# Attention, gated unit and rational unit on one core: the matrices of batches 3 to 7 from half-precision parts of the weights

## The chip, the cores and the metric

One core of one Trainium2 chip runs the whole kernel. The metric is the device time of one execution in microseconds; a kernel's time is the median of its runs.

## The reference, cut to what matters

There are 8 batches of 8 heads with 576 rows of 64, 32 packing rows a head, a gated unit of width 1536 and a second unit of width 2048.

```python
p_packed = sm_attn(p, k, v)                # 32 rows a head
out = sm_attn(q, p_packed, p_packed)       # 576 rows a head
x = transposed out                          # 4608 x 512
xn = x / rms * rms_g
g, val = xn @ w_gate, xn @ w_val           # 512 x 1536 each
x = silu(g) * val @ w_out                  # 1536 x 512
h = x @ w_in                               # 512 x 2048
out = (P(h) / (Q(h) + 1e-6)) @ w_out2      # polynomials in h; 2048 x 512
```

Since the second attention only mixes the 32 packed rows of each head, a row of x is a row of weights (8 heads x 32) times the packed rows. The kernel therefore multiplies the packed rows with `w_gate` and `w_val` once a batch and applies the attention's weights to the products. These products are what the kernel calls the matrices of a batch.

## The kernel before

Most products are taken in three passes in half precision: each operand is a high part and a low part (`PASSES`: high by high, high by low, low by high), summed in PSUM. The 64-bit inputs of the weights are decoded into single precision by three VectorE instructions (L129, L133, L135, the steps wB, wC and wD).

The work of a batch is written as short steps with names, and a list of names fixes the order in which every engine gets its instructions. `START` (L904) holds batches 0 and 1; `BLOCK` (L959) is run for b = 2 to 6 (L1233) and joins the gated unit of batch b with the attention and the matrices of batch b + 1; batch 7 has a loop of its own (L1253). The second unit follows. TensorE's queue and the others are served in the order of the list.

The steps that matter here:

- G and V followed by half and column (`gv_mm`, L982): a projection, six half-precision matmuls into one of five PSUM tiles of the pool `ps_m`. A is the tanh (ScalarE, L1001), D and E are the two products (VectorE, L1005 and L1008), which read and so free the tiles of G and V; Y and Z are the high and low part of the result (ScalarE L1015, GpSimd L1020).
- O followed by half, column group and third (`o1_mm`, L1049): the product with `w_out`; P, Q and S evict and store it.
- hk, hv, hq are casts of the next batch's inputs (ScalarE, L700), lk, lv, zq their low parts (VectorE L709 or GpSimd L707).
- bA and bD write the packed rows of a batch as high and low parts into `pkz` (L785, L791); bM (`pk_gain`, L800) writes them once more in single precision, times the gain of the norm, into `pkm` by four small VectorE instructions (L260).
- M0 to Mb (`m_mm`, L380) are the 12 items of the matrices. An item takes 512 columns of `w_gate` or `w_val` and 128 rows of two weight tiles. Its two matmuls write the two halves of 64 partitions of a PSUM tile, and both operands are in single precision:

```python
for i_ in range(2):
    nc.tensor.matmul(
        out=ps[64 * i_:64 * i_ + 64, :], lhsT=pkm[g][:, i_, :], rhs=wgv[nm, fr, 2 * g + i_], start=True, stop=True
    )
```

  MA and MD (L388, L393) take an item out of PSUM as a high part (ScalarE, L391) and a low part (VectorE, L396).
- wB to wL prepare the 32 weight tiles of the second unit: wL loads a raw tile (ScalarE's queue, one of three buffers), wB, wC, wD decode it, wA scales (L1184) and wH casts (L1188) on ScalarE, wP takes the low part on GpSimd (L1192), wS stores both parts to DRAM on ScalarE's queue. `w2.start()` (L1232) issues the first three loads ahead of block 2. Seven tiles are done in each of blocks 2 and 3 and six in each of blocks 4 to 6.

In `BLOCK`, the steps of TensorE around the M items stand in this order (M0, M2, M4, the five from M1 to M7, M8 M9 and Mb Ma are six groups):

```text
G13 M0 V13 M2 G14 V14 G15 V15 G16 bm1 V16 G17 M4 V17 M1 M3 M5 M6 M7 G18 V18 ... G1b M8 M9 V1b Mb Ma O100
```

A first-attention step (L588) multiplies in single precision, s1a (L732) and xo (L853) multiply in half precision with 64 columns in places.

Of the kernel before, what the change touches and what calls it, by code (L numbers as in the profile page):

```python
# [9 lines left out]
F32 = mybir.dt.float32  # L10
F16 = mybir.dt.float16
I32 = mybir.dt.int32
I64 = mybir.dt.int64
AF = mybir.ActivationFunctionType
ALU = mybir.AluOpType
# [5 lines left out]
PASSES = ((0, 0), (0, 1), (1, 0))  # L21
S_QKP = 2.0**4
S_V = 2.0**7
S_A = 2.0**12
S_PK = 2.0**10
S_AN = 2.0**5
S_M = 2.0**13
# [3 lines left out]
S_WI2 = 2.0**10  # L31
S_G = 2.0**4
S_WO2 = 2.0**11
# [3 lines left out]
def attention_pack_glu_rational_kernel(  # L37
# [16 lines left out]
    nc = tc.nc  # L54
# [5 lines left out]
    KC = DM // 128  # L60
# [17 lines left out]
    act = nc.scalar.activation  # L78
    stt = nc.vector.scalar_tensor_tensor
# [6 lines left out]
    const = sb("const", "left")  # L86
    st_p = sb("stage", "left")
# [12 lines left out]

    g_raw = const.tile([128, KC], F32, name="g_raw")
    g_sc = const.tile([128, KC], F32, name="g_sc")
    g_first = const.tile([128, KC], F32, name="g_first")
    m_half = const.tile([128, 2], F32, name="m_half")
    ab = const.tile([128, 6], F32, name="ab")
# [3 lines left out]
    wgv = {}  # L109
# [54 lines left out]
    def place1(nm, fr, kc):  # L164
        t = wgv[nm, fr, kc] = gv_p.tile([128, 512], F32, name=f"w{nm}_{fr}_{kc}")
        return t

    w1 = Weights(w_items, place1)
    w1_dec = w1.steps()
# [24 lines left out]
    m_items = [(fr, nm, g) for fr in range(DFF // 512) for nm in "gv" for g in range(2)]  # L194
# [14 lines left out]
    pkz = [at_p.tile([128, 2, 4, 64], F16, name=f"pkz{g}") for g in range(2)]  # L209

    pkm = [at_p.tile([128, 2, 64], F32, name=f"pkm{g}") for g in range(2)]
# [3 lines left out]
    pT = at_p.tile([128, 2, 4, 64], F16, name="pT")  # L215
# [161 lines left out]
    def matrices(b, st):  # L377


        def m_mm(i):  # L380
            fr, nm, g = m_items[i]
            ps = st["mm", i] = ps_m.tile([128, 512], F32, tag="m", name="mm")
            for i_ in range(2):
                nc.tensor.matmul(  # L384
                    out=ps[64 * i_:64 * i_ + 64, :], lhsT=pkm[g][:, i_, :], rhs=wgv[nm, fr, 2 * g + i_], start=True, stop=True
                )

        def m_hi(i):  # L388
            fr, nm, g = m_items[i]
            t = mt[b, nm, fr, g] = mt_p.tile([128, 2, 512], F16, tag="mt", bufs=MTB, name="mt")  # L390
            act(out=t[:, 0], in_=st["mm", i], func=AF.Copy, scale=1.0)  # L391

        def m_lo(i):  # L393
            fr, nm, g = m_items[i]
            t = mt[b, nm, fr, g]
            stt(  # L396
                out=t[:, 1], in0=st["mm", i], scalar=1.0, in1=t[:, 0], op0=ALU.mult,
                op1=ALU.subtract,
            )

        def m_less(i):
            fr, nm, g = m_items[i]
            for i_ in range(2):
                nc.tensor.matmul(
                    out=st["mm", i][64 * i_:64 * i_ + 64, :], lhsT=minus[:, 64 * i_:64 * i_ + 64],
                    rhs=mt[b, nm, fr, g][:, 0], start=False, stop=True,
                    skip_group_check=True,
                )

        def m_rest(i):  # L410
            fr, nm, g = m_items[i]
            act(out=mt[b, nm, fr, g][:, 1], in_=st["mm", i], func=AF.Copy)

        pieces = {}
        for i in range(len(m_items)):
            for nm, f in (("M", m_mm), ("MA", m_hi), ("MD", m_lo), ("MP", m_less), ("ML", m_rest)):
                pieces[f"{nm}{i:x}"] = lambda f=f, i=i: f(i)
        return pieces
# [221 lines left out]
    def attention(b):  # L640
# [316 lines left out]
        "+MAa +MDa"  # L957
    )
    BLOCK = (  # L959
# [19 lines left out]
    )  # L979


# [162 lines left out]
    def norms():  # L1144
        nc.vector.tensor_scalar_mul(minus, ident, -1.0)
        nc.vector.tensor_scalar_mul(g_sc, g_raw, S_M / (S_A * S_V))
        nc.vector.tensor_scalar_mul(g_first, g_raw, S_M / S_A)

    def constants():
# [10 lines left out]
    w2_items = []  # L1160
# [4 lines left out]
        w2_items.append(("o", 0, kc, w_out2[kc * 128:(kc + 1) * 128, :]))  # L1165
    w2_dram = {it[:3]: tc.dram_tile((128, 2, 512), F16, name="w2{}_{}_{}".format(*it[:3])) for it in w2_items}
    w2t = {}
    kept = []

    def place2(nm, fr, kc):  # L1170

        raw = w2.raw[[it[:3] for it in w2_items].index((nm, fr, kc))]
        t = raw.bitcast(F16)[:, 0:1024].rearrange("p (a t) -> p a t", a=2)
        kept.append(((nm, fr, kc), t))
        return t, S_WI2 if nm == "i" else S_WO2

    w2 = Weights(w2_items, place2)

    w2_done = []

    def w2_scale():
        w2_done.append(w2.dec.pop(0))
        nm = w2.items[len(w2_done) - 1][0]
        act(out=w2_done[-1], in_=w2_done[-1], func=AF.Copy, scale=S_WI2 if nm == "i" else S_WO2)  # L1184

    def w2_hi():
        t, _ = place2(*w2.items[w2.n][:3])
        act(out=t[:, 0], in_=w2_done[-1], func=AF.Copy)  # L1188

    def w2_lo():  # L1190
        t = kept[-1][1]
        nc.gpsimd.tensor_tensor(out=t[:, 1], in0=w2_done[-1], in1=t[:, 0], op=ALU.subtract)  # L1192
        w2.n += 1

    def w2_store():
        key, t = kept.pop()
        nc.scalar.dma_start(out=w2_dram[key], in_=t)

    w2_dec = w2.steps()

    def w2_pieces(b):
        todo = {nm: lambda: next(w2_dec) for nm in ("wB", "wC", "wD")}
        todo |= {"wA": w2_scale, "wH": w2_hi, "wP": w2_lo, "wS": w2_store, "wL": w2.load}
        return {f"{nm}{j}": f for nm, f in todo.items() for j in range(7 if b < 4 else 6)}

    w2_p = None
    w2_left = list(w2_items)
# [14 lines left out]
    ctx.enter_context(tc.manual_schedule())  # L1222
    steps = {"-" + nm: f for nm, f in attention_first().items()}
    steps |= attention(1) | block(0) | w1_pieces() | blanks() | {"cc": norms, "cd": constants}
    steps |= {"+" + nm: f for nm, f in (attention(2) | block(1) | w2_pieces(1)).items()}
    for nm in START.split():
        steps[nm]()
    an.pop(0)
# [2 lines left out]
        ys.pop((b, h, c))  # L1231
    w2.start()  # L1232
    for b in range(2, B - 1):  # L1233
        steps = attention(b + 1) | block(b) | w2_pieces(b)
        for nm in BLOCK.split():
            if nm in steps:
                steps[nm]()
            else:
                assert nm[0] == "w", nm
        an.pop(b)  # L1240
        for h in range(2):
            for c in range(NF1):
                ys.pop((b, h, c))
# [6 lines left out]
    steps = block(B - 1)  # L1250
    chunks = [f"{h}{c:x}" for h in range(2) for c in range(NF1)] + [None]
    before = None
    for x in chunks:  # L1253
# [9 lines left out]
            steps["E" + x]()  # L1263
            w2_load()
        before = x
    assert not w2_left and w2.n == len(w2_items)
    last1 = itertools.chain(out1_slots(B - 1, 0), out1_slots(B - 1, 1))
    an_p.release()
    mt_p.release()
# [181 lines left out]
```

## Time and profile before

| | us |
|---|---|
| median of 3 runs | 1603.7 |
| lowest and highest run | 1601.66, 1603.87 |
| the profiled execution | 1598.39 |
| its span, first to last instruction | 1596.6 |

The profile is of one execution, and its times are measured from the span's start. PE is TensorE, PEld its weight loads, DVE VectorE, ACT ScalarE, POOL GpSimd, SP SyncE; a q behind a name is the queue of the engine. Matmul records are pipelined: a record lasts longer than the time until the next one may start, so times between starts tell more than durations. A single-precision matmul of the program is two records. Blocks 2 to 6 begin at 281.83, 380.00, 476.32, 573.26 and 670.36 us, and the loop of batch 7 at 765.73.

### The profile page before, as it was taken

What the parts mean: (1) busy time and instruction counts of PE and PEld (TensorE: products, weight loads), DVE (VectorE), ACT (ScalarE), POOL (GpSimd) and SP (SyncE); (2) the same over time, 40 slices, a digit from 0 to 9 for tenths busy, and PEclk for the clock granted to TensorE, in tenths of its full rate; (3) what the DMA queues carried; (4) which work ended last, traced back from release to release, by engine and by line L of the source; (5) the groups of instructions that cost most, each with busy time, mean ns of one, the idle gap of its engine ahead of it and who ended that gap; (6) DMA issues with size and microseconds to landing.
All of it is one profiled execution on the core that took longest, in us unless ns stands there. A gap on an engine that the chain in (4) does not pass through costs nothing.

```text
span 1596.6 us, 26777 instructions
## 1 busy us (share of the span) xinstructions
PE 1535.1 (96%) x10020; PEld 896.5 (56%) x10020; DVE 1284.2 (80%) x2184; ACT 918.9 (58%) x1847; POOL 541.7 (34%) x639
## 2 busy tenths in 40 slices
PE   6788999999999999999999999999999999999998
PEld 4365776757667576676765444444444444444443
DVE  6898755786767867578579998989898989898980
ACT  3556464665746657566466656566556566565650
POOL 1022132343523425144334333334333334343430
PEclk7899999999999999999999999999999999999999
DMA  8766562676876648374710001010101010100000
GB/s 253 218 173 141 118 132 45 150 184 118 180 156 150 157 112 199 96 162 91 254 37 17 31 1 53 1 53 1 53 1 53 1 54 0 54 1 27 1 27 27
DMA packets 221906, 142.98 MB, mean 90 GB/s; under 512 B 162256, under 2 KB 199120, under 8 KB 220624
## 3 DMA queue, kind: packets, MB, share of 16 engines
q1 hardware_dynamic: 188528, 107.84, 27.7%
q10 hardware_dynamic: 33152, 33.43, 7.5%
q8 instruction: 78, 1.28, 0.3%
q14 instruction: 52, 0.43, 0.1%
q0 software_dynamic: 96, 0.01, 0.0%
HBM read 82.32 MB, written 27.26 MB: 69 GB/s over the span
## 4 chain that ended last, share of the span: by engine, by line
PE 76%; DVE 11%; DMA 7%; ACT 2%; issue 2%; ACTq 1%; POOL 0%; SPq 0%; POOLq 0%; DVEq 0%
PE h L1296 22%; PE o L1367 21%; PE o L1051 14%; PE gv L990 12%; PE mm L384 4%; PE xo L853 1%; DMA raw<-in_moe_w_val_dram 1%; DMA w2i<-raw 1%; DMA w2o<-raw 1%; DVE t L1005 1%; DVE t L1008 1%; DMA raw<-in_moe_w_gate_dram 1%; DVE w L1326 1%; ACTq L1043 1%; DMA x2s<-x2e 1%
## 5 line engine op out<-in xcount | busy, mean ns | idle before, releaser
L1367 PE MATMUL o<-w2o,g 128*128 128x512 f16 x1728 | 397.0, 380 | 7.0 <-DVE osb L1361 3.8
L1296 PE MATMUL h<-xi,w2i 128*128 128x512 f16 x1728 | 396.3, 379 | 0.0
L990 PE MATMUL gv<-an,mt 128*128 128x256 f16 (+1 forms) x2304 | 301.0, 288 | 10.7 <-DVE t L1005 9.0
L1367 PEld LDWEIGHTS <-g 128*128 128x128 f16 x1728 | 169.1, 98 | 214.0 <-issue 7.4
L1296 PEld LDWEIGHTS <-w2i 128*128 128x128 f16 x1728 | 169.1, 98 | 201.0
L1051 PE MATMUL o<-y,wo 128*128 128x256 f16 (+1 forms) x2160 | 273.0, 285 | 6.8 <-DVE wo L178 3.8
L990 PEld LDWEIGHTS <-mt 128*128 128x128 f16 x2304 | 221.6, 98 | 98.4 <-issue 42.9
L1051 PEld LDWEIGHTS <-wo 128*128 128x128 f16 x2304 | 222.8, 98 | 73.3 <-issue 7.2
L1311 POOL TENSOR_SCALAR w<-ah,cf 128x512 f32<-128x512 f32 x144 | 111.2, 773 | 374.4 <-DVE t L1328 150.4
L1020 POOL TENSOR_TENSOR y<-t,y 128x256 f16<-128x256 f32 (+1 forms) x180 | 139.7, 777 | 287.3 <-ACT y L1015 283.8
L1334 POOL TENSOR_TENSOR g<-t,g 128x512 f16<-128x512 f32 x144 | 174.5, 1212 | 98.1 <-issue 70.2
L1308 ACT ACTIVATE ah<-h 128x512 f32<-128x512 f32 x144 | 85.6, 594 | 204.9 <-PE h L1296 204.8
L1326 DVE SCALAR_TENSOR_TENSOR w<-w,r 128x512 f32<-128x512 f32 x144 | 178.9, 1242 | 4.0 <-ACT r L1325 4.0
L1316 DVE TENSOR_TENSOR w<-w,ah 128x512 f32<-128x512 f32 x144 | 135.6, 942 | 0.0
L1314 DVE TENSOR_TENSOR t<-t,h 128x512 f32<-128x512 f32 x144 | 98.5, 684 | 42.7 <-ACT t L1309 42.4
L1309 ACT ACTIVATE t<-h,cf 128x512 f32<-128x512 f32 x144 | 111.5, 774 | 23.6 <-POOL g L1334 23.6
L1315 DVE SCALAR_TENSOR_TENSOR t<-t,cf,h 128x512 f32<-128x512 f32 x144 | 107.7, 748 | 5.1
L1001 ACT ACTIVATE t<-gv 128x256 f32<-128x256 f32 (+1 forms) x192 | 77.7, 405 | 56.1 <-PE gv L990 50.9
L1327 DVE SCALAR_TENSOR_TENSOR t<-t,cf,r 128x512 f32<-128x512 f32 x144 | 107.5, 746 | 0.0
L1015 ACT ACTIVATE y<-t 128x256 f16<-128x256 f32 (+1 forms) x180 | 78.8, 439 | 44.1 <-DVE t L1008 42.0
L1005 DVE SCALAR_TENSOR_TENSOR t<-t,gv 128x256 f32<-128x256 f32 (+1 forms) x192 | 86.0, 448 | 22.3 <-ACT t L1001 20.7
L1328 DVE SCALAR_TENSOR_TENSOR t<-w,t 128x512 f32<-128x512 f32 x144 | 99.6, 692 | 4.9
(177 smaller groups left out, 1705.3 us busy)
## 6 DMA issues: line engine op xcount, KB each, us to landing
xi<-x2s SPq DMA_DIRECT2D x9, 1024.0 KB, 5.6
raw<-in_k_dram SPq DMA_DIRECT2D x16, 512.0 KB, 5.8
raw<-in_v_dram SPq DMA_DIRECT2D x16, 512.0 KB, 4.8
raw<-in_q_dram SPq DMA_DIRECT2D x16, 512.0 KB, 5.3
raw<-in_moe_w_in_dram ACTq DMA_DIRECT2D x16, 512.0 KB, 4.8
raw<-in_moe_w_out_dram ACTq DMA_DIRECT2D x16, 512.0 KB, 4.2
out_dram<-osb SPq DMA_DIRECT2D x32, 256.0 KB, 2.5
raw<-in_moe_w_gate_dram SPq DMA_DIRECT2D x12, 512.0 KB, 4.9
```

Source lines behind the costliest of these rows:

```text
L990: nc.tensor.matmul(out=ps, lhsT=mt[b, nm, c // 4, g][:, l, cs], rhs=an[b][:, 2 * r_ + g, cols], start=(n == 0), stop=(n == 5))
L1020: nc.gpsimd.tensor_tensor(out=y[:, 1], in0=t, in1=y[:, 0], op=ALU.subtract)
L1051: nc.tensor.matmul(out=ps, lhsT=wo1[c][:, l, d * 128:(d + 1) * 128], rhs=ys[b, h, c][:, r_, :], start=(c == 0 and n == 0), stop=(c == NF1 ...
L1296: nc.tensor.matmul(out=ps, lhsT=w[:, l, cs], rhs=x2in[j][:, r_, kc, :], start=(n == 0), stop=(n == 3 * KC - 1))
L1309: act(out=t, in_=ps, func=AF.Identity, scale=cf[:, 0:1], bias=cf[:, 7:8])
L1311: nc.gpsimd.tensor_scalar(out=w, in0=ah, scalar1=cf[:, 6:7], scalar2=cf[:, 5:6], op0=ALU.mult, op1=ALU.add)
L1315: stt(out=t, in0=t, scalar=cf[:, 1:2], in1=ps, op0=ALU.add, op1=ALU.mult)
L1316: nc.vector.tensor_tensor(out=w, in0=w, in1=ah, op=ALU.mult)
L1326: stt(out=w, in0=w, scalar=Q1, in1=r0, op0=ALU.add, op1=ALU.mult)
L1327: stt(out=t, in0=t, scalar=cf[:, 2:3], in1=r0, op0=ALU.add, op1=ALU.mult)
L1334: nc.gpsimd.tensor_tensor(out=g[:, 1], in0=t, in1=g[:, 0], op=ALU.subtract)
L1367: nc.tensor.matmul(out=ps, lhsT=gs[j, c][:, l, t * 128:(t + 1) * 128], rhs=w2t["o", 0, c][:, r_, :], start=(c == 0 and n == 0), stop=(c == ...
```

## The change

For batches 3 to 7 the M items are taken in three half-precision passes from `pkz` and from parts of the weights. The parts take the place of the single-precision weights: 1024 half-precision numbers a partition fit where 512 single-precision ones were. In block 2, after batch 2's items, 24 tiles are split: CH casts the tile times the gain (`g_half`, a new constant) into a temporary tile (ScalarE), CL writes the low part into the first half of the tile's place (VectorE), CC copies the high part into the second half (GpSimd). There are two temporary tiles. The steps bM are gone from the orders of blocks 2 to 6. All 32 tiles of the second unit are prepared in blocks 3 to 6, eight in each. Block 2 has an order of its own (`SPLITS`), and `BLOCK` is reordered.

```diff
+S_WGV = 2.0**10
...
+    SPLIT = 3
+
+    def parts_of(w):
+
+        return w.bitcast(F16).rearrange("p (a t) -> p a t", a=2)
+
+    def gv_split():
+
+        tmp, steps = {}, {}
+
+        def hi(i, w, kc):
+            t = tmp[i] = st_p.tile([128, 512], F32, tag="raw32", bufs=2, name="parts").bitcast(F16)[:, 0:512]
+            act(out=t, in_=w, func=AF.Copy, scale=g_half[:, kc:kc + 1])
+
+        def lo(i, w, kc):
+            stt(out=parts_of(w)[:, 0], in0=w, scalar=g_half[:, kc:kc + 1], in1=tmp[i], op0=ALU.mult, op1=ALU.subtract)
+
+        def keep(i, w):
+            nc.gpsimd.tensor_copy(out=parts_of(w)[:, 1], in_=tmp.pop(i))
...
             for i_ in range(2):
-                nc.tensor.matmul(
-                    out=ps[64 * i_:64 * i_ + 64, :], lhsT=pkm[g][:, i_, :], rhs=wgv[nm, fr, 2 * g + i_], start=True, stop=True
-                )
+                w, pr = wgv[nm, fr, 2 * g + i_], slice(64 * i_, 64 * i_ + 64)
+                if b < SPLIT:
+                    nc.tensor.matmul(out=ps[pr, :], lhsT=pkm[g][:, i_, :], rhs=w, start=True, stop=True)
+                    continue
+                for n, (l, r_) in enumerate(PASSES):
+                    nc.tensor.matmul(
+                        out=ps[pr, :], lhsT=pkz[g][:, l, 3 * i_, :], rhs=parts_of(w)[:, 1 - r_, :], start=(n == 0), stop=(n == 2)
+                    )
+
+        sc = 1.0 if b < SPLIT else S_M / (S_PK * S_WGV)
...
-            act(out=t[:, 0], in_=st["mm", i], func=AF.Copy, scale=1.0)
+            act(out=t[:, 0], in_=st["mm", i], func=AF.Copy, scale=sc)
...
+        nc.vector.tensor_scalar_mul(g_half, g_raw, S_WGV)
...
-        return {f"{nm}{j}": f for nm, f in todo.items() for j in range(7 if b < 4 else 6)}
+        todo["wL"] = w2.load
+        steps = {f"{nm}{j}": f for nm, f in todo.items() for j in range(8)}
+        for nm, f in (("wA", w2_scale), ("wH", w2_hi), ("wP", w2_lo), ("wS", w2_store)):
+            for j in range(8):
+                steps[f"{nm}{j}"] = lambda f=f, n=8 * (b - SPLIT) + j: f(n)
+        return steps
...
-        steps = attention(b + 1) | block(b) | w2_pieces(b)
-        for nm in BLOCK.split():
+        steps = attention(b + 1) | block(b) | (gv_split() if b == 2 else w2_pieces(b))
+        for nm in (SPLITS if b == 2 else BLOCK).split():
```

The first and the last line of the two new orders, as strings of the diff:

```diff
+    SPLITS = (
+        "G00 pl hk00 hk01 V00 lk00 A00 G01 lk01 hk02 lk02 V01 hv00 D00 G02 A01 E00 hv01 lk03 V02 D01 A02 G03 E01 "
...
+        "O132 MAb xr2 MDb nA20 P13 nD20 Q13 nT20 S13"
...
+        "G00 pl hk00 wB0 wC0 hk01 V00 A00 G01 lk00 hk02 D00 V01 hv00 E00 G02 A01 lk01 Y00 lk02 V02 hv01 Z00 D01 "
...
+        "wS6 wP7 S12 O131 nT11 xq20 wS7 xr2 O132 nA20 P13 nD20 wL6 Q13 nT20 S13 wL7"
```

TensorE's steps around the M items stand in these orders in `SPLITS` and in the new `BLOCK`:

```text
SPLITS: G13 M0 V13 M2 G14 V14 ... G17 M4 V17 bm1 G18 ... G1a V1a M1 M3 M5 M6 cm0 cm1 cm2 G1b V1b O100 O101 O102 O110 M7 O111 O112 xm00 xm01 M8 O120 M9 O121 xm10 xm11 O122 O130 Ma O131 xm20 Mb O132
BLOCK:  G13 V13 M0 M2 G14 V14 G15 V15 bm1 G16 V16 G17 V17 M1 M3 M4 M5 M6 M7 G18 V18 ... G1b V1b Ma Mb M8 M9 O100
```

The decoding steps of the new `BLOCK` stand at these places: wB0 wC0 at its head, wD0 to wD2 among O00 to O03, tiles 3 and 4 between G10 and G18, tiles 5 to 7 from O102 on. In the old one wB5 and wC5 stood between G18 and G1b, and the rest of tile 5 and tile 6 (of blocks 2 and 3) among the last O steps.

## Rows read from the trace of the kernel before

**Rows 1.** The page: shares of the chain that ended last, by engine

```profile
PE 76%; DVE 11%; DMA 7%; ACT 2%; issue 2%; ACTq 1%; POOL 0%; SPq 0%; POOLq 0%; DVEq 0%
```

**Rows 2.** Windows, blocks 2 to 6: stretch, length, PE, PEld, DVE, ACT, POOL busy, clock, DMA

```profile
281.83:380.00 98.17, 94.30 (x800) 67.31 (x799) 73.05 (x161) 60.65 (x142) 37.55 (x47) 0.98 0.72 164
380.00:476.32 96.32, 93.30 (x800) 66.42 (x798) 71.82 (x160) 59.91 (x142) 37.00 (x47) 1.00 0.74 156
476.32:573.26 96.94, 93.30 (x800) 66.37 (x798) 70.28 (x158) 59.19 (x140) 35.56 (x46) 1.00 0.62 149
573.26:670.36 97.10, 93.21 (x801) 66.44 (x799) 70.39 (x157) 59.26 (x140) 35.51 (x46) 1.00 0.60 146
670.36:765.73 95.37, 93.12 (x800) 66.49 (x798) 70.19 (x157) 59.11 (x140) 35.12 (x46) 1.00 0.53 114
```

**Rows 3.** Timeline of the head of block 2: start us, us, engine, line, instruction

```profile
281.83 3.45 PE L990 MATMUL gv<-an,mt 128*128 128x256 f16 x30
...
283.02 1.67 ACTq L148 DMA_DIRECT2D raw<-in_moe_w_in_dram  x3
...
284.74 1.15 ACT L700 ACTIVATE x16in<-raw 128x512 f16<-128x512 f32 x2 [1.14 <-issue]
285.80 0.37 ACT L1001 ACTIVATE t<-gv 128x256 f32<-128x256 f32 x1
...
287.28 0.43 DVE L129 TENSOR_SCALAR raw<-raw 128x512 int32<-128x512 int32 x1 [2.96 <-DMA raw<-in_moe_w_in_dram]
...
289.15 7.04 PE L990 MATMUL gv<-an,mt 128*128 128x256 f16 x48 [3.87 <-DVE t L1005]
```

**Rows 4.** Windows: the three us after the wait of rows 3

```profile
289.00:292.00 3.00, 2.85 (x14) 2.04 (x14) 2.69 (x9) 1.54 (x5) 0.67 (x1) 0.52 0.05 18
```

**Rows 5.** Timeline of TensorE, block 6: two matrix steps in a row

```profile
738.00 1.94 PE L384 MATMUL mm<-wg,pkm 128*64 128x512 f32 x8
739.87 0.99 PE L990 MATMUL gv<-an,mt 128*128 128x320 f16 x6
```

**Rows 6.** Timeline of TensorE, block 4: a matrix step alone

```profile
518.77 1.08 PE L384 MATMUL mm<-wg,pkm 128*64 128x512 f32 x4
519.78 0.99 PE L990 MATMUL gv<-an,mt 128*128 128x320 f16 x6
```

**Rows 7.** Timeline of TensorE: two halves in turn, half precision (block 4)

```profile
508.19 0.84 PE L732 MATMUL s1a<-kT,pT 128*64 128x512 f16 x6
508.86 0.26 PE L741 MATMUL s1b<-kTt,pT 128*64 128x64 f16 x6
```

**Rows 8.** Timeline of TensorE: one half alone, single precision (first attention)

```profile
73.13 1.03 PE L588 MATMUL first<-pkN,eT 128*64 128x256 f32 x4
```

**Rows 9.** VectorE's groups of block 4: busy us, mean ns, idle before

```profile
L133 DVE SCALAR_TENSOR_TENSOR raw<-raw,raw 128x512 int32<-128x512 int32 x6 | 5.0, 838 | 0.1
...
L135 DVE SCALAR_TENSOR_TENSOR raw<-raw,raw 128x512 int32<-128x512 int32 x6 | 4.7, 786 | 0.1
...
L129 DVE TENSOR_SCALAR raw<-raw 128x512 int32<-128x512 int32 x6 | 2.6, 433 | 0.0
```

**Rows 10.** Nearest rows of the new steps: one line's durations, min/median/max ns

```profile
L174 ACT ACTIVATE wo<-raw x12: 629/630/632, 82.0 to 123.5; 128x512 f16<-128x512 f32 x12
...
L178 DVE SCALAR_TENSOR_TENSOR wo<-raw,wo x12: 674/684/970, 82.8 to 124.3; 128x512 f16<-128x512 f32 x12
...
L1192 POOL TENSOR_TENSOR raw<-raw,raw x32: 1149/1160/1503, 307.3 to 751.0; 128x512 f16<-128x512 f32 x32
...
L1219 POOL MEMSET pkz<- x2: 525/534/544, 65.2 to 65.6; 128x512 f16 x2
```

**Rows 11.** The same view of a decoding instruction, blocks 2 to 6

```profile
L133 DVE SCALAR_TENSOR_TENSOR raw<-raw,raw x32: 684/693/1527, 287.7 to 734.6; 128x512 int32<-128x512 int32 x32
```

**Rows 12.** Windows of block 4: a dense stretch and the stretch after it

```profile
516.30:536.30 20.00, 20.00 (x144) 10.47 (x143) 18.98 (x41) 17.07 (x39) 13.07 (x15) 1.00 0.75 177
556.30:572.30 16.00, 14.85 (x112) 10.59 (x110) 4.32 (x12) 6.72 (x17) 3.70 (x7) 1.00 0.65 135
```

More of the change, by code (lines that the diff above doesn't have):

```diff
@@ L102, in attention_pack_glu_rational_kernel @@
     g_sc = const.tile([128, KC], F32, name="g_sc")
+    g_half = const.tile([128, KC], F32, name="g_half")
     g_first = const.tile([128, KC], F32, name="g_first")
@@ L166, in place1 @@
         return t
+    SPLIT = 3
[10 more added lines that the diff above has]
+            nc.gpsimd.tensor_copy(out=parts_of(w)[:, 1], in_=tmp.pop(i))
+        for i, (fr, nm, g) in enumerate(m_items):
+            for e in range(2):
+                n, kc = 2 * i + e, 2 * g + e
+                w = wgv[nm, fr, kc]
+                steps[f"CH{n}"] = lambda n=n, w=w, kc=kc: hi(n, w, kc)
+                steps[f"CL{n}"] = lambda n=n, w=w, kc=kc: lo(n, w, kc)
+                steps[f"CC{n}"] = lambda n=n, w=w: keep(n, w)
+        return steps
     w1 = Weights(w_items, place1)
@@ L396, in m_lo @@
             stt(
-                out=t[:, 1], in0=st["mm", i], scalar=1.0, in1=t[:, 0], op0=ALU.mult,
+                out=t[:, 1], in0=st["mm", i], scalar=sc, in1=t[:, 0], op0=ALU.mult,
                 op1=ALU.subtract,
@@ L958, in attention_pack_glu_rational_kernel @@
     )
+    SPLITS = (
[20 rows of a table added]
+    )
     BLOCK = (
         "G00 pl hk00 wB0 wC0 hk01 V00 A00 G01 lk00 hk02 D00 V01 hv00 E00 G02 A01 lk01 Y00 lk02 V02 hv01 Z00 D01 "
[18 rows of a table removed]
[18 rows of a table added]
     )
@@ L1167, in attention_pack_glu_rational_kernel, with w2_scale, w2_hi, w2_lo @@
     w2t = {}
[L1168 to L1177, printed above, removed]
+    w2 = Weights(w2_items, None)
     w2_done = []
-    def w2_scale():
+    w2_parts = {}
+    def w2_scale(n):
         w2_done.append(w2.dec.pop(0))
[L1183 to L1197, printed above, removed]
+        act(out=w2_done[n], in_=w2_done[n], func=AF.Copy, scale=S_WI2 if w2.items[n][0] == "i" else S_WO2)
+    def w2_hi(n):
+        t = w2_parts[n] = w2.raw[n].bitcast(F16)[:, 0:1024].rearrange("p (a t) -> p a t", a=2)
+        act(out=t[:, 0], in_=w2_done[n], func=AF.Copy)
+    def w2_lo(n):
+        t = w2_parts[n]
+        nc.gpsimd.tensor_tensor(out=t[:, 1], in0=w2_done[n], in1=t[:, 0], op=ALU.subtract)
+    def w2_store(n):
+        nc.scalar.dma_start(out=w2_dram[w2.items[n][:3]], in_=w2_parts.pop(n))
     w2_dec = w2.steps()
@@ L1202, in w2_pieces @@
         todo = {nm: lambda: next(w2_dec) for nm in ("wB", "wC", "wD")}
-        todo |= {"wA": w2_scale, "wH": w2_hi, "wP": w2_lo, "wS": w2_store, "wL": w2.load}
-        return {f"{nm}{j}": f for nm, f in todo.items() for j in range(7 if b < 4 else 6)}
+        todo["wL"] = w2.load
[3 more added lines that the diff above has]
+                steps[f"{nm}{j}"] = lambda f=f, n=8 * (b - SPLIT) + j: f(n)
+        return steps
     w2_p = None
@@ L1224, in attention_pack_glu_rational_kernel @@
     steps |= attention(1) | block(0) | w1_pieces() | blanks() | {"cc": norms, "cd": constants}
-    steps |= {"+" + nm: f for nm, f in (attention(2) | block(1) | w2_pieces(1)).items()}
+    steps |= {"+" + nm: f for nm, f in (attention(2) | block(1)).items()}
     for nm in START.split():
@@ L1265, in attention_pack_glu_rational_kernel @@
         before = x
-    assert not w2_left and w2.n == len(w2_items)
+    assert not w2_left and len(w2_done) == len(w2_items) and not w2_parts
     last1 = itertools.chain(out1_slots(B - 1, 0), out1_slots(B - 1, 1))
```

53 rows, old and new, of tables (BLOCK, SPLITS) are left out of this document.

## The prediction, made before the changed kernel was run

> **What bounds the kernel now.** I read the page's chain first: 76% of the time that set the end is TensorE's, 11% VectorE's [rows 1]. The change works in blocks 2 to 6 alone, so the next view is one window for each [rows 2]: 95.4 to 98.2 us long, TensorE busy for 93.1 to 94.3 of them and without work for 3.87, 3.02, 3.64, 3.89 and 2.25 us. A block therefore becomes shorter by TensorE time taken out of it or by these waits, as long as VectorE (70 to 73 us) can follow. The timeline at the head of block 2 [rows 3] shows its one wait: 30 projection matmuls fill the five PSUM tiles; VectorE stands until 287.28 at its first decoding step of a second-layer weight (the load, issued at 283.02, hasn't landed), and D00, which would free a PSUM tile, is queued behind that step. TensorE goes on only at 289.15 and has the granted clock 0.52 for the next three microseconds [rows 4], its lower level (1.2 GHz); before it fell, the engine had stood for 3.87 us.
>
> **The matrix steps (M).** Two items in a row hold TensorE from 738.00 to 739.87, 1.87 us [rows 5]; one alone from 518.77 to 519.78, 1.01 us [rows 6]. So one more item costs 0.86 us and leaving the group 0.15. An item is two single-precision matmuls, one a 64-column half; each is two records, so the x4 of a lone item is all of it. Eight records of 592 ns or more in 1.94 us run two at a time.
>
> The new item is six half-precision matmuls, three of half 0 and then three of half 1. Its nearest row has the same shape but the halves in turn: s1a's six take 0.67 us to the start of the next line [rows 7], three slots of 0.223. Whether halves issued one after the other also overlap is the point on which the sum turns. Four single-precision records of one half alone, with 256 columns, take 1.03 us and so follow each other [rows 8]: records of one half do not pair. The old item issues half 0's two records and then half 1's, and still runs in pairs [rows 5]; so a record of half 1 starts ahead of one of half 0 that was issued before it and waits. The new order asks for the same past two waiting matmuls instead of one; I take it that this works: 0.67 us an item. The bounds are 0.67 and six slots in series, 1.34; 0.67 is taken because the old item, the nearest row in its order, overlaps fully.
>
> The Trainium skill ("TensorE: Matmul & The Clock Gate", Part 3, The mechanism) says otherwise: only weight loads are pulled ahead, and matmuls start and end strictly in program order. Rows 5 and 8 together do not agree with it for column halves; its price is the second rival's.
>
> Gain: 12 x (0.86 - 0.67) = 2.3 us a block. The order of TensorE's steps also changes: M steps stood in six groups a block and now stand in three (M0 M2; M1 M3 M4 M5 M6 M7; Ma Mb M8 M9), which saves 3 x 0.15 = 0.45; in block 2's new order they stand in nine, which costs 0.45.
>
> **pk_gain goes.** Four small VectorE instructions a block; counted at nothing. The M steps now wait for the low part of pkz instead, which stood just before.
>
> **Second-layer weights.** Seven decodings leave block 2; block 3 gets one more and blocks 4 to 6 two more. One costs VectorE 0.838 + 0.786 + 0.433 = 2.06 us [rows 9], so block 2 loses 14.4 and blocks 4 to 6 gain 4.1 each. On ScalarE two more mean four activations of 0.63 (by the same shape, [rows 10]) and four DMA issues of 1.67/3 = 0.56 [rows 3]: 4.8 us on an engine that idles for 36 of 97 [rows 2]; on GpSimd 2 x 1.16 [rows 10], of 60 idle. TensorE's work covers all three. Without that cover the 4.1 us would lengthen a block, and the waits term below stands for the share that does. One place to watch: the last load of a block waits on ScalarE's queue for the store of the same buffer, and the next block's first tanh is behind it. No row shows this wait; between nothing and 4.3 us (283.02 to 287.28, a load's issue to its user [rows 3]) I take nothing, since the evictions of the last output tile lie between.
>
> **Block 2's head.** With the decoding gone, D00 waits for the first tanh alone, which ends at 286.17 behind three load issues and the first casts [rows 3]. Three residual steps stand ahead of D00 on VectorE, and ScalarE delivers the last of their casts at 285.89, so D00 ends near 287.0 (an estimate: two steps of 0.4 us after that) and TensorE, which runs out at 285.28, stands about 1.8 us instead of 3.87: -2.1. The half-speed stretch lost 3 x 0.48 = 1.4 us [rows 4]; with half the wait I take -1.0 (bounds 0 and -1.4).
>
> **The split in block 2.** 24 times a ScalarE cast (0.63), a VectorE subtraction (0.68 to 0.97) and a GpSimd copy (between the fill's 0.53 and the subtraction's 1.16) [rows 10]. VectorE: 73.05 - 14.4 + 16.4 = 75 us, up to 82, of some 95; ScalarE 61 + 15 - 9 = 67; GpSimd 38 - 8 + 13 to 28. All three lie beside TensorE, but each M step now waits for a chain through three engines and two temporary tiles. No row shows that wait: nothing, to all of the 5.0 us that the block otherwise gains and more; I take +1.5.
>
> The decoding step, with both inputs in SBUF, lasts 684 ns at least and up to 1527 [rows 11]. The Trainium skill ("SBUF — State Buffer", Who interferes with whom) has a rule that fits: a VectorE instruction with two SBUF inputs and a GpSimd one that reads SBUF block each other. By it the new copies and subtractions collide; the price by rows is in the first rival.
>
> **Waits in blocks 3 to 6.** In the dense stretch of block 4 VectorE is busy for 18.98 of 20 us, in a later one for 4.32 of 16 [rows 12]. Eight of the twelve M items stand in the dense part, where TensorE becomes faster. The new order moves decoding out of it (steps 5 to 7 now stand in the last output tiles), so I let the waits grow by only 0.3 us a block.
>
> **Sum.** Blocks 3 to 6: -2.3 - 0.45 + 0.3 = -2.4 each, -9.8. Block 2: -2.3 + 0.45 - 2.1 - 1.0 + 1.5 = -3.4. One small constant (g_half) before the first block: +0.1, at most 0.2. Together -13.1. The profiled execution took 1598.4 us (span 1596.6), so it would take 1585.3; the median of the runs is 5.3 us above it, 1603.7, so I forecast **1591**. Its own range is 1584 to 1597: the first end has no new wait in block 2, the whole of the clock's 1.4 and the waits of blocks 3 to 6 shrinking a little; the other has only one waiting matmul passed, an extra slot of 0.22 for each of 21 groups, 4.7 us.
>
> **First rival: VectorE takes over.** If it cannot follow in the dense stretch, the eight items there save nothing: 4 x 8 x 0.19 = 6.1 us lost, 1597. If besides each of the 24 subtractions is stretched by 1.527 - 0.684, block 2 has 95 us of VectorE work and gains nothing: about 1601. For it: 18.98 of 20; against it: the moved decoding and the 16 us in which VectorE is mostly free.
>
> **Second rival, the slower side: program order holds.** Half 1's first matmul then starts only beside half 0's last: four slots an item, 0.89 us, and one more a group, 0.22. Blocks 3 to 6: 12 x 0.03 + 3 x 0.22 - 0.45 + 0.3 = +0.9 each; block 2: 0.4 + 2.0 + 0.45 - 3.1 + 1.5 = +1.2. Together +4.8, so 1608. This is the rule of the Trainium skill turned into time. It decides if passing two waiting matmuls fails where passing one works. At its worst no halves overlap: 60 x 0.48 = 29 us, some 1628. Against it stand rows 5 and 8.
>
> **How the numbers follow.** Forecast 0.65; VectorE 0.19; program order 0.13; no overlap 0.03. 0.2% is 3.2 us, about what a measurement of this kernel can tell from no change. The forecast lies beyond it (0.65), the first rival mostly (0.15 of 0.19), program order mostly on the other side (0.08 of 0.13, the rest within). So faster 0.80, same 0.09, slower 0.11. The range of 1583 to 1604 takes in the forecast, the first rival and the lightest of the second; some 0.17 is left outside.
>
> **What would show it.** Right: a lone M item of six half-width records less than 0.85 us long, two in a row under 1.5; blocks 3 to 6 near 94 us; no wait on a load at block 2's head and no clock of 0.52 behind it. Wrong: records of one half alone in TensorE's timeline; a wait of M on GpSimd's copies; TensorE waiting longer than 4 us a block on D and E steps; subtractions near 1.5 us.

## The result and the profile after

The changed kernel takes 1588.57 us (median of 4 runs, 1584.87 to 1589.01), the kernel before in the same comparison 1602.68 (4 runs, 1600.85 to 1603.87): a ratio of 0.9908, with the interval 0.9889 to 0.9927. The profiled execution took 1584.87 us with a span of 1583.1. Against the profiled execution of before that is -13.5 us; the sum of the prediction was -13.1. Both profiled executions were faster than the other runs of their kernel named here.

The page's chain first, which answers to [rows 1]: shares of the chain that ended last, by engine.

```profile
PE 77%; DVE 12%; DMA 6%; ACT 2%; issue 2%; ACTq 1%; SPq 0%; POOLq 0%; DVEq 0%; POOL 0%
```

TensorE bounds the kernel as before. The windows of blocks 2 to 6 answer to [rows 2]: stretch, length, busy PE, PEld, DVE, ACT and POOL, clock, share of the DMA engines, GB/s moved.

```profile
280.64:375.20 94.56, 90.79 (x824) 67.21 (x823) 78.93 (x160) 68.16 (x152) 47.44 (x64) 1.00 0.54 115
375.20:468.36 93.16, 89.77 (x825) 67.87 (x822) 72.57 (x159) 60.20 (x143) 39.75 (x48) 1.00 0.69 153
468.36:564.14 95.78, 90.04 (x825) 67.83 (x822) 72.92 (x159) 60.98 (x145) 39.33 (x48) 1.00 0.72 167
564.14:657.78 93.64, 90.10 (x824) 67.88 (x822) 73.17 (x159) 60.13 (x145) 38.91 (x48) 1.00 0.72 167
657.78:752.25 94.47, 89.72 (x824) 67.92 (x822) 74.16 (x160) 60.33 (x145) 39.03 (x48) 1.00 0.63 146
sum 471.61, PE 450.42 PEld 338.71 DVE 371.75 ACT 309.80 POOL 204.44; mean PE 90.08 PEld 67.74 DVE 74.35 ACT 61.96 POOL 40.89
```

Set beside [rows 2], the blocks are 3.61, 3.16, 1.16, 3.46 and 0.90 us shorter, 12.3 together. Another 1.2 lies ahead of block 2, where both kernels run the same instructions but for one small constant; block 2 began between 280.64 and 285.64 us in the eleven profiled executions beside before's 281.83, so this part is chance. What follows block 6 lasts 830.9 in both.

In blocks 3 to 6 TensorE is busy for 89.7 to 90.1 us instead of 93.1 to 93.3, 3.3 less on the average. Length less busy time is the wait: 3.39, 5.74, 3.54 and 4.75 us, where it was 3.02, 3.64, 3.89 and 2.25. So the work shrank by more than the blocks did, and 1.2 us a block came back as waiting. The list of what TensorE waited for in blocks 2 to 6 (us in total, times, longest) says for what:

```profile
PE gv L1051 <- DVE t L1066: 13.5, 9, 3.0
PE xo L891 <- DMA eT<-a: 6.1, 4, 2.1
```

gv on DVE t is a projection waiting for a product of the gated unit (D, now L1066) to free a PSUM tile; xo waits for the transposed second attention of the next batch. No M step is in the list. The same list of before, for blocks 3 to 6:

```profile
PE gv L990 <- DVE t L1005: 5.1, 8, 0.9
PE mm L384 <- DVE t L1005: 3.9, 3, 1.7
PE mm L384 <- DVE pkm L260: 1.6, 2, 1.4
PE xo L853 <- DMA eT<-a: 1.1, 1, 1.1
```

In these four blocks M's waits for VectorE (3.9 and 1.6) are gone, and more has come elsewhere. xo waits 5.0 us more. All eight waits of gv in before stand at the block heads, 5.1 us; in after the heads have 7.1 (1.12, 3.00, 1.20 and 1.80), and two waits for a later D, 1.49 and 1.32 in blocks 5 and 6, are new.

The matrix steps themselves, on TensorE's timeline (start us, us, engine, line, instruction), answer to [rows 5, 6]:

```profile
354.58 0.84 PE L420 MATMUL mm<-wv,pkz 128*64 128x512 f16 x6
355.36 2.89 PE L1112 MATMUL o<-y,wo 128*128 128x320 f16 x20
...
514.39 0.84 PE L420 MATMUL mm<-wg,pkz 128*64 128x512 f16 x6
515.07 0.82 PE L420 MATMUL mm<-wv,pkz 128*64 128x512 f16 x6
515.82 3.66 PE L1051 MATMUL gv<-an,mt 128*128 128x320 f16 x24
...
523.97 0.84 PE L420 MATMUL mm<-wg,pkz 128*64 128x512 f16 x6
...
527.98 2.21 PE L1051 MATMUL gv<-an,mt 128*128 128x320 f16 x15
```

A lone item takes 0.78 us from its start to the next line's (1.01 before), two take 1.43 (1.87 before), six 4.01. That is 0.65 an item and 0.13 to leave the group. Six matmuls in 0.65 us are three slots of 0.217: the halves overlap, although the program issues three of half 0 and then three of half 1.

The head of block 2, which answers to [rows 3], on the timeline of all engines:

```profile
280.64 3.45 PE L1051 MATMUL gv<-an,mt 128*128 128x256 f16 x30
...
284.22 1.09 DVE L747 SCALAR_TENSOR_TENSOR x16in<-raw,x16in 128x256 f16<-128x256 f32 x3 [1.08 <-ACT x16in L738]
...
285.23 0.41 DVE L1066 SCALAR_TENSOR_TENSOR t<-t,gv 128x256 f32<-128x256 f32 x1
...
285.69 4.09 PE L1051 MATMUL gv<-an,mt 128*128 128x256 f16 x36 [1.60 <-DVE t L1066]
...
289.29 1.15 DVE L691 SCALAR_TENSOR_TENSOR a<-praw,a 32x512 f16<-32x512 f32 x1
...
290.71 0.40 DVE L1066 SCALAR_TENSOR_TENSOR t<-t,gv 128x256 f32<-128x256 f32 x1
...
291.16 1.58 PE L1051 MATMUL gv<-an,mt 128*128 128x256 f16 x13 [1.38 <-DVE t L1066]
```

D00 no longer stands behind a load: TensorE waits 1.60 us instead of 3.87. But the five projections after that run out too, since VectorE has low parts of the attention's inputs (L747, L691) ahead of the next D, and a wait of 1.38 follows.

The place that the prediction said to watch is the end of a block on ScalarE's queue. The same view at the head of block 4:

```profile
468.36 2.78 PE L1051 MATMUL gv<-an,mt 128*128 128x256 f16 x24
469.76 0.51 ACT L904 ACTIVATE n<-d,rms 64x256 f16<-64x256 f32 x1 [3.12 <-DMA an<-n]
469.82 0.34 ACTq L150 DMA_DIRECT2D raw<-in_moe_w_in_dram  x1
...
471.29 1.21 ACTq L1104 DMA_DIRECT2D x2s<-x2e  x2
...
472.60 0.56 ACTq L150 DMA_DIRECT2D raw<-in_moe_w_in_dram  x1
473.20 1.15 ACT L738 ACTIVATE x16in<-raw 128x512 f16<-128x512 f32 x2 [2.61 <-DVE raw L135]
474.26 0.36 ACT L1062 ACTIVATE t<-gv 128x256 f32<-128x256 f32 x1
...
475.13 1.03 PE L1051 MATMUL gv<-an,mt 128*128 128x256 f16 x8 [3.00 <-DVE t L1066]
```

ScalarE's last steps of block 3 are still in its queue when block 4 begins on TensorE: the norm step nA20 waits 3.12 us for a transpose, two weight loads and the store are issued behind it, and only then come the first casts and the first tanh, at 474.26. TensorE stands for 3.00 us. The last load, which the prediction named, is itself hardly held up: it is issued at 472.60, right behind the store's two issues.

### The profile page after: what moved, and what is told of

The parts are those of the page before. It is cut to its first block, busy times and chain, and to the rows that moved or that the text cites. A ratio compares the mean times of both kernels' runs of the same rounds, so it can differ in the third digit from the quotient of the medians.

```text
span 1583.1 us, 27080 instructions
## 1 busy us (share of the span) xinstructions
PE 1516.0 (96%) x10140; PEld 900.3 (57%) x10140; DVE 1300.1 (82%) x2189; ACT 930.1 (59%) x1871; POOL 563.5 (36%) x663
## 4 chain that ended last, share of the span: by engine, by line
PE 77%; DVE 12%; DMA 6%; ACT 2%; issue 2%; ACTq 1%; SPq 0%; POOLq 0%; DVEq 0%; POOL 0%
PE h L1353 22%; PE o L1424 21%; PE gv L1051 14%; PE o L1112 13%; PE mm L420 2%; DMA eT<-a 2%; PE mm L417 1%; PE xo L891 1%; DVE t L1066 1%; PE pk L811 1%; DMA raw<-in_moe_w_val_dram 1%; DMA raw<-in_moe_w_gate_dram 1%; DVE w L1383 1%; DVE t L1069 1%; DVE v L747 1%
## 5 line engine op out<-in xcount | busy, mean ns | idle before, releaser
L1051 PE MATMUL gv<-an,mt 128*128 128x256 f16 (+1 forms) x2304 | 297.1, 286 | 15.0 <-DVE t L1066 13.8
L1066 DVE SCALAR_TENSOR_TENSOR t<-t,gv 128x256 f32<-128x256 f32 (+1 forms) x192 | 85.8, 447 | 24.9 <-ACT t L1062 23.9
L1381 ACT ACTIVATE r<-w,one 128x512 f32<-128x512 f32 x144 | 103.3, 717 | 0.0
```

The source lines that it names most:

```text
L1051: nc.tensor.matmul(out=ps, lhsT=mt[b, nm, c // 4, g][:, l, cs], rhs=an[b][:, 2 * r_ + g, cols], start=(n == 0), stop=(n == 5))
```

## The experiments

Theory: the time falls because half precision makes each M item shorter, and because the new order keeps VectorE's work out of M's way; of the expected gain, waits at the block heads and before xo take some back. Rivals: the order alone does it; half precision alone does it; the split is not hidden in block 2; the gain is mostly block 2's lost decoding.

### The new order with single-precision items (e1_single_m)

```diff
-                if b < SPLIT:
+                if True:
                     nc.tensor.matmul(out=ps[pr, :], lhsT=pkm[g][:, i_, :], rhs=w, start=True, stop=True)
...
-        sc = 1.0 if b < SPLIT else S_M / (S_PK * S_WGV)
+        sc = 1.0
```

CH, CL and CC are taken out of `SPLITS`, and bM0 and bM1 stand behind bD0 and bD1 in both orders.

> The changed kernel's orders with the M steps back in single precision (pk_gain's four instructions again, no split of the weights in block 2). If the gain is TensorE time of the M steps, 60 items take 0.86 instead of 0.65 us again, 12.6 us, of which shorter waits give back some 1 us a block: 8 to 12 us slower than the changed kernel, about 1597 to 1600, with the head of block 2 still at about 1.6 us of waiting. If the gain comes from the new order and the moved decodings, the time stays within 3 us of the changed kernel's 1588.6.

Measured: 1614.1 us (6 runs, 1610.58 to 1615.3) beside 1605.18 for before (23 runs): 1.0058, interval 1.0038 to 1.0079. So the order alone is slower than the kernel before, and half precision is worth some 24 us on top of it, twice what I had expected. The sum of the windows of its five blocks (columns as above):

```profile
sum 493.05, PE 469.29 PEld 336.96 DVE 357.03 ACT 295.84 POOL 183.94; mean PE 93.86 PEld 67.39 DVE 71.41 ACT 59.17 POOL 36.79
```

The five blocks are 21.4 us longer than after's, of which TensorE's busy time makes 18.9 and the waits (length less busy time) 2.6. To take this apart I read the windows of M's line alone (stretch, length, PE busy, PEld busy, clock and DMA as above). Block 4 of before, of this kernel and of after, in this order:

```profile
476.32:573.26 96.94, 11.84 (x48) 2.82 (x48) 1.00 0.62 149
```

```profile
479.46:581.73 102.27, 10.96 (x48) 3.17 (x48) 0.97 0.68 155
```

```profile
468.36:564.14 95.78, 8.36 (x72) 4.12 (x72) 1.00 0.72 167
```

Here bringing the items together saves 0.88 us of M, half precision another 2.60. In block 2, whose items stand apart, half precision saves 2.8. Over the five blocks M's line falls from 56.35 us to 43.34, which makes 13.0 of the 18.9. The other 5.9 fit the clock, whose mean is 0.97 to 0.98 in blocks 3 to 5, where after's is 1.00. The window on the first such stretch, and TensorE's largest new wait in the five blocks:

```profile
459.86:463.27 3.41, 3.41 (x17) 2.38 (x18) 2.59 (x7) 2.58 (x7) 0.00 (x0) 0.57 0.25 50
```

```profile
PE xo L891 <- DMA eT<-a: 10.3, 4, 3.9
```

At 459.86 a wait of 3.48 for xo's transpose ends, and the granted clock is 0.57, near the lower level, for the 3.41 us after it: 3.41 x 0.43 = 1.5 us lost. There are four such stretches, behind waits of 3.48, 2.62, 3.87 and 2.08 us, 5.7 us lost in all by the same sum, and after's profile has none in its blocks. My expectation had counted M's time and no new waits. That the order alone is slower than before, although it makes M shorter by 0.88 us in block 4, has the same two causes: in blocks 2 to 6 it waits 23.8 us (493.05 less 469.29), before 16.7 by [rows 2], and loses the clock behind the longest waits.

### Half-precision items in the old order (e2_old_order)

`BLOCK` gets the order of before, without bM0 and bM1 and with the steps of tile 7 added at the end; `SPLITS` and everything else are after's.

```diff
-        "at1 hv11 M0 lv10 lv11 Y12 M2 lv12 hv12 Z12 MA0 lv13 G14 lv14 MA2 D13 A14 L E13 sq10 V14 D14 Y13 MD0 G15 "
...
+        "wB3 bA0 aD1 Y10 V11 A11 Z10 bD0 G12 hv10 D11 hv11 V12 E11 bt0 A12 G13 Y11 lv10 hv12 D12 at1 Z11 M0 wL1 "
+        "E12 A13 lv11 S03 V13 Y12 D13 MA0 lv12 Z12 M2 E13 MD0 G14 Y13 lv13 MA2 Z13 V14 lv14 A14 MD2 sq10 G15 L "
```

> The changed kernel with the old order in blocks 3 to 6 (the eighth tile of the second unit added at the end). If the order is worth its three groups of M steps less and the decoding moved out of the dense stretch, blocks 3 to 6 become 0.8 to 1.5 us longer each: 1592 to 1595. If the order is what the gain rests on, they lose 2.5 us each and the time is 1598 or more; if it is worth nothing, 1588 to 1590.

Measured: 1601.83 us (12 runs, 1596.7 to 1605.56): 0.9984, interval 0.9968 to 1.0. Of the 14 us only 2.6 are left, and the interval reaches to nothing. TensorE's waits in blocks 3 to 6:

```profile
PE gv L1051 <- DVE t L1066: 8.7, 6, 3.2
PE mm L420 <- DVE t L1066: 8.4, 6, 3.5
PE gv L1051 <- DVE mt L434: 6.5, 5, 1.6
```

Two lines are here that after does not have: the items wait for D (8.4 us; 3.9 in before) and the projections for MD (6.5; 0.8 in before), all on VectorE. The windows of block 4 (columns as above) hold both:

```profile
515.60:535.60 20.00, 19.66 (x179) 12.08 (x178) 17.99 (x34) 15.21 (x36) 12.24 (x14) 1.00 0.80 185
535.60:555.60 20.00, 15.52 (x150) 9.90 (x150) 15.86 (x30) 9.73 (x20) 4.35 (x5) 0.91 0.62 162
```

In the first 20 us VectorE is busy for 17.99 and TensorE runs ahead of it; in the next 20 TensorE stands for 4.48. This is the first rival of the prediction, in the old order: the shorter items are given back as waits for VectorE. How much of it the items make is not taken apart, since this run also decodes eight tiles a block, where before has six or seven. Part of the loss is the clock again, whose mean is 0.97 in block 4 and 0.98 in block 6. In after the same 20 us of block 4, counted from its start, hold 17.19 us of VectorE's work, before 18.98 [rows 12], and TensorE works for 19.93 of them:

```profile
508.40:528.40 20.00, 19.93 (x191) 13.02 (x188) 17.19 (x37) 17.03 (x41) 12.58 (x15) 1.00 0.77 164
```

Together with e1_single_m the four corners are, each against before: order alone +8.9 us, half precision alone -3.4 by the medians (-2.6 by the ratio), both -14.1. The two parts need each other. Neither corner is one change alone: both have the new block 2, and the second unit's tiles in blocks 3 to 6, which no run takes apart. xo's wait belongs to the new order and not to half precision: it is 10.3 us in e1_single_m and 0.7 here.

### Without the split (e3_no_split)

The 72 steps CH, CL and CC are left out, and the items of batches 3 to 7 multiply parts of `w_out` instead of the parts that are never written; the rest is as in after.

```diff
-                        out=ps[pr, :], lhsT=pkz[g][:, l, 3 * i_, :], rhs=parts_of(w)[:, 1 - r_, :], start=(n == 0), stop=(n == 2)
+                        out=ps[pr, :], lhsT=pkz[g][:, l, 3 * i_, :], rhs=wo1[2 * g + i_][:, r_, :], start=(n == 0), stop=(n == 2)
```

> The steps CH, CL and CC of block 2 are left out, and the M steps of batches 3 to 7 read the parts of w_out instead of the split weights (same shapes). If the split lies beside TensorE's work, as the trace after says (3.8 us of waits in block 2, of which 1.6 at its head come from the load issues), block 2 becomes at most 2 us shorter: 1586.5 to 1589. If it is a burden (the first rival's price in block 2), it becomes 4 us shorter or more: below 1585.

Measured: 1589.8 us (6 runs): 0.9903, interval 0.9879 to 0.9927, the same as after. Block 2 lasts 94.29 us instead of 94.56, with TensorE's waits of 1.60, 1.38 and 0.60 in the same places. The split is hidden. After's view of CL's line (min, median and max ns; then who waited for it, us and times) shows the chain through three engines at work without TensorE in it:

```profile
L185 DVE SCALAR_TENSOR_TENSOR wg<-wg,g_half,parts x12: 731/746/1093, 297.9 to 360.0; 128x512 f16<-128x512 f32 x12
...
  POOL wv L188: 6.0, 7
  POOL wg L188: 6.0, 4
```

GpSimd waited 12.0 us for the subtractions, but no M step waited for GpSimd.

### Before, with one decoding moved (e5_before_late_decode)

In the kernel before, wB0 and wC0 of block 2 go from the head to just ahead of wD0.

```diff
-        for nm in BLOCK.split():
+        order = BLOCK
+        if b == 2:
+            order = order.replace("wB0 wC0 ", "").replace("wD0 ", "wB0 wC0 wD0 ")
+        for nm in order.split():
```

> The kernel before, with the first two decoding steps of block 2 moved from its head to the place of the third. If the wait at the head came from the load alone, it falls from 3.9 to about 1.6 us and the half-clock stretch behind it goes or shrinks: 2 to 3.7 us faster than before. If the wait only moves to another step, no difference.

Measured: 1601.22 us (12 runs): 0.9982, interval 0.997 to 0.9995. Block 2 falls from 98.17 to 96.11 us; its head wait is 1.39 with another of 0.51 behind it, and the stretch of half clock [rows 4] is gone. So about 3 us of the change's gain (2.9 by the ratio, 0.8 to 4.8 by its interval) was to be had without the change, by moving two steps.

### The halves further apart (e4_halves_apart)

In blocks 3 to 6 the pairs M0 M2, Ma Mb and M8 M9 issue six matmuls of half 0 and then six of half 1.

```diff
-                for n, (l, r_) in enumerate(PASSES):
+                half = lambda ps=ps, pr=pr, g=g, i_=i_, w=w: [
...
+                if b > SPLIT and i in (0, 2, 8, 9, 10, 11) and i_ == 1:
+                    st.setdefault("second", []).append(half)
+                    if i in (2, 9, 11):
+                        for f in st.pop("second"):
+                            f()
+                else:
+                    half()
```

> In blocks 3 to 6 the pairs of items M0 M2, Ma Mb and M8 M9 issue six matmuls of half 0 and then six of half 1. If TensorE lets half 1 start past any number of waiting matmuls of half 0, a pair still takes 1.43 us to the next projection (six slots of 0.216). If it looks past no more than two, the first matmul of half 1 starts three slots late: about 2.1 us a pair. If halves overlapped only at a change of half, eleven slots, 2.4 us.

Measured in a single execution: 1587.45 us, too few to price the edit as a whole. TensorE's timeline of a pair:

```profile
516.08 0.86 PE L420 MATMUL mm<-wg,pkz 128*64 128x512 f16 x4
516.75 0.38 PE L420 MATMUL mm<-wv,pkz 128*64 128x512 f16 x1
516.78 0.38 PE L420 MATMUL mm<-wg,pkz 128*64 128x512 f16 x1
516.97 0.38 PE L420 MATMUL mm<-wv,pkz 128*64 128x512 f16 x1
517.00 0.38 PE L420 MATMUL mm<-wg,pkz 128*64 128x512 f16 x1
517.18 0.84 PE L420 MATMUL mm<-wv,pkz 128*64 128x512 f16 x4
517.96 2.21 PE L1060 MATMUL gv<-an,mt 128*128 128x320 f16 x15
```

The program's order is three of wg (half 0), three of wv (half 0), three of wg (half 1), three of wv (half 1). The first line has four of wg: the fourth belongs to half 1 and starts ahead of all three of wv that were issued before it. So a matmul of the other half passes three that wait, and that is shown here by the order itself. It doesn't pass four: then half 1 would have begun a slot earlier. The pair takes 1.88 us where after's takes 1.43, 0.45 more: two slots of 0.217, which are those in which half 0 runs alone. The value lies between the 1.43 and the 2.1 that had been expected for the two cases.

### Block-end steps carried over the head (t1_head, t1_again, after_again)

The last store, load and norm steps of a block are issued behind the first tanh steps of the next one.

```diff
+    kept, LATE = {}, ["S13", "wL7", "nA20", "nD20", "nT20"]
     for b in range(2, B - 1):
         steps = attention(b + 1) | block(b) | (gv_split() if b == 2 else w2_pieces(b))
-        for nm in (SPLITS if b == 2 else BLOCK).split():
+        steps |= {"<" + nm: f for nm, f in kept.items()}
+        kept = {nm: steps[nm] for nm in LATE if nm in steps}
+        for nm in (SPLITS if b == 2 else BLOCK).split() + (LATE if b == B - 2 else []):
...
-        "wS6 wP7 S12 O131 nT11 xq20 wS7 xr2 O132 nA20 P13 nD20 wL6 Q13 nT20 S13 wL7"
+        "G00 pl hk00 wB0 wC0 hk01 V00 A00 <S13 G01 lk00 hk02 D00 V01 hv00 E00 G02 A01 <wL7 <nA20 lk01 Y00 lk02 "
+        "V02 hv01 Z00 D01 G03 A02 E01 pA lk03 V03 D02 Y01 G04 E02 A03 <nD20 <nT20 Z01 pD hv02 V04 Y02 D03 G05 A04 "
...
+        "nD11 wL5 nT10 wH7 Q12 xm20 wS6 wP7 S12 O131 nT11 xq20 wS7 xr2 O132 P13 wL6 Q13"
```

> The changed kernel with the last store of a block, its last weight load and the last part of the attention's weights (S13, wL7, nA20, nD20, nT20) issued behind the first tanh steps of the next block. If these steps, ahead of the first tanh on ScalarE, make the waits at the heads of blocks 3 to 6 (1.12, 3.00, 1.20 and 1.80 us), most of the 7.1 us goes: 3 to 7 us faster than the changed kernel. If the casts hk alone make them, or the time comes back as a wait further on, less than 2 us.

Measured: 1582.12 us (6 runs, 1580.86 to 1586.8): 0.9866, interval 0.9843 to 0.9889. Since after had been timed on another chip, both ran once more, side by side.

> The changed kernel itself, beside the next run on the same chip, since the two were so far only compared through the kernel before. Theory (block heads cost the new order 5 to 7 us): 12 to 17 us below the kernel before, and 5 to 8 us above the next kernel. Rival (the difference between the two was chance between chips): both within 3 us of each other.

> The changed kernel with the last store, load and norm steps of a block carried behind the first tanh steps of the next one, on the same chip as the changed kernel. Theory: 5 to 8 us below it. Rival: within 3 us of it.

Measured, beside 1605.58 for before (11 runs): after 1590.8 us (6 runs, 1586.47 to 1592.1; 0.9913, interval 0.9889 to 0.9937), this version 1584.66 (6 runs, 1581.28 to 1587.39; 0.9869, interval 0.9845 to 0.9893). It is 6.1 us faster than after, and after's gain over before is found again. The waits of t1_head's blocks 2 to 6:

```profile
PE gv L1051 <- DVE t L1066: 8.5, 10, 1.6
PE xo L891 <- DMA eT<-a: 5.4, 4, 1.6
```

gv's waits fall from 13.5 to 8.5, the longest from 3.0 to 1.6, which is block 2's. The longest wait at the head of block 4 is 0.73 us where it was 3.00. That these steps held up the tanh is thereby shown, for all five together; which of them does it was not taken apart.

### The second attention later, and everything at once (t2_later_x, t3_all)

```diff
-        "O102 cx2 wL4 cy2 MDa tA1 xm00 wB5 ce2 xm01 P10 tD1 xq00 O110 Q10 tT1 xq01 cn2 co2 S10 O111 xr0 wC5 wD5 "
+        "O102 cx2 wL4 cy2 MDa tA1 wB5 ce2 P10 tD1 O110 xm00 xm01 xq00 Q10 tT1 xq01 cn2 co2 S10 O111 xr0 wC5 wD5 "
```

> The changed kernel with the two steps xm00 and xm01, and the square of the first, one output third (1.6 us) later in blocks 3 to 6. If the waits on the transposed weights (2.14, 1.57, 0.79 and 1.58 us) come from TensorE arriving too early, they shrink by up to 1.6 each: 3 to 5 us faster. If the transposes themselves come later by as much, or the next link of the attention's chain waits instead, no difference.

Measured: 1590.74 us (6 runs): 0.9909, interval 0.9884 to 0.9933, no gain. In blocks 2 to 6 xo's wait falls by 4.9 us to 1.2, as meant. gv's rises by 2.8 to 16.3, at the block heads: at block 4 nA20, the last of the norm steps that follow xo, begins 1.89 us behind the block's start, in after 1.40. The heads of blocks 4 and 6 stand for 3.55 and 3.04 us, both with a stretch of half clock behind. That the later norm steps alone make this is not shown. t3_all joins the three edits (D13 is also moved to behind Y12).

> Both of these, and D13 ahead of the residual parts of the values (the waits of 1.49 and 1.32 us in blocks 5 and 6). If the three kinds of wait are separate, the sum of what they cost goes: 8 to 13 us faster than the changed kernel, 1576 to 1581. If one is behind another, about as much as the best of the two alone.

Measured: 1582.43 us (5 runs, 1577.19 to 1583.69): 0.9856, interval 0.9832 to 0.9881. It is not told apart from t1_head, though its five blocks are the shortest of all, 463.4 us together against 466.4 and after's 471.6; its first block began 1.9 us later than t1_head's.

## Why the prediction was right

The forecast was 1591 and the measured median 1588.57, within the range; the profiled execution came out at 1584.87, where the sum gave 1585.3. That it came so near is in part luck: the 1.2 us ahead of block 2 are chance, and errors of the parts cancel. By its steps:

- **The matrix steps.** Right, and the point on which it turned is shown: the halves overlap past two waiting matmuls, and e4_halves_apart shows that past three they still do. The Trainium skill ("TensorE: Matmul & The Clock Gate", Part 3, The mechanism) has matmuls start and end strictly in program order; the trace does not agree, with six matmuls in 0.65 us and the fourth record of wg ahead of the first of wv. So the second rival falls. The size was a little low: 2.75 us a block for items and groups were forecast, TensorE's work fell by 3.3. By M's own line in block 4, half precision gave 2.60 (forecast 2.3) and the grouping 0.88 (forecast 0.45); that line also counts the modelled ends that overlap the next line, so it shows a little more than TensorE's work lost.
- **Waits in blocks 3 to 6.** This is the term that was mis-sized: +0.3 us a block were forecast, +1.2 measured (3.20 to 4.36 on the average). Its reason was only half right. That the new order keeps VectorE from taking over is shown by e2_old_order, where with the old one it does take over; that the moved decoding is what does it was not tested by itself. But the new waits are elsewhere: xo 5.0 us more in the four blocks, a later D 2.8, the block heads 2.0, against 5.5 less before the M items. xo stands nowhere in the prediction, and why the new order makes TensorE wait there stays open. For the heads the prediction named the place ("the last load of a block waits on ScalarE's queue") and put nothing on it, within bounds of nothing and 4.3. It is the norm step nA20 on that queue that waited, 3.12 in block 4. The runs of t1_head put the steps at the block ends at 6.1 us, more than the heads grew, since before's heads waited too.
- **The two errors together.** Blocks 3 to 6 gave -8.7 where -9.8 was forecast: 0.6 a block too little work saved in the forecast, 0.9 too little waiting.
- **Block 2.** -3.6 measured, -3.4 forecast, by parts that were each off. The head wait came as forecast (1.60 us, 1.8 forecast). The half-clock stretch went altogether, as the larger bound had it. The +1.5 for the split's chain was wrong: e3_no_split puts it at 0.3. In its place came waits of 1.38 and 0.59 that the forecast did not have; they stand in e3_no_split as well, so the split is not their cause. TensorE's waits in the block are 3.77 us together, 3.87 before.
- **First rival.** VectorE is busy for 78.93 of 94.56 us in block 2 (75 to 82 were forecast) and no M step waited for the split. The subtractions lasted 731 to 1285 ns, with medians of 746 and 752, and not 1.5 us. It came true only for the old order.
- **Two sums.** By the prediction's own terms the worst case of the second rival is 1591 + 60 x 0.67 = 1631, not 1628, and the slow end of its own range 1591 + 4.7 = 1596, not 1597. Its fast end needs the waits of blocks 3 to 6 to shrink by 1.2 us a block, which the prediction calls a little.

What stays open: after's profiled execution shows no half-clock stretch in its blocks, but the one of after_again has one behind the same wait at block 4's head, 2.95 us long. How much of e1_single_m's 5.9 us from the clock a median run of it has, one profile doesn't say.

## What to carry to other kernels

A shorter step in a stretch where another engine is nearly full was worth little here in the old order, so cost the order and the step together and test each alone. At the seam of two blocks read the in-order queue of the engine that opens the next block (here ScalarE): late norm steps, stores and loads at its end are paid for at the next head. Where the two column halves of the array work side by side, alternate them in short turns: three in a row on one half cost nothing here, six in a row two slots.

## What had not been expected of the hardware

A matmul on one column half starts ahead of up to three waiting ones of the other half and not ahead of four: 1.43 us for a pair whose halves lie three apart, 1.88 for six apart.

Waits of TensorE of about the same length do not always end at the same granted clock. Behind waits of 2.08, 2.62, 3.48 and 3.87 us the clock went to its lower level (1.2 GHz) in e1_single_m, and behind one of 2.03 at the head of block 6 there it stayed at the higher (2.4 GHz). Behind one of 3.00 at block 4's head in after it stayed at the higher (granted 1.00 in the 3 us that follow), and behind 2.95 at the same place in after_again it fell (0.50).
